# A new order, engine choice and bank choice for periods two to eight of a fused attention and channel-mix kernel

## The chip, the cores and the metric

The kernel runs on one core of a Trainium2 chip. The metric is the device time of one execution in microseconds (us). The kernel before took 204.27 us, the median of three runs (202.83 to 205.34). Engines are named as in the profile: PE (TensorE matmuls), PEld (TensorE weight loads), DVE (VectorE), ACT (ScalarE), POOL (GpSimd) and SP (SyncE, which here only issues DMAs).

## What is computed

Eight batches, eight heads, 576 tokens, head size 64; then a channel mix with 512 channels and 1024 hidden ones. Without casts and reshapes:

```python
kv  = einsum('bhsd,bhse->bhde', k, v)
out = einsum('bhsd,bhde->bhse', q, kv)
x   = out / sqrt(mean(out * out, -1) + 1e-6) * g_norm      # heads side by side: (8, 576, 512)
xk  = mu_k * x + (1 - mu_k) * x_prev                       # x_prev: one token earlier, zeros first
xr  = mu_r * x + (1 - mu_r) * x_prev
kk  = maximum(xk @ w_k, 0)
result = sigmoid(xr @ w_r) * ((kk * kk) @ w_v)
```

## The kernel before, in words

The work is cut into small steps, and the table ORDER at the top of the file writes out their order by hand, in eight strings that I call periods. Each word of it is one step: a name, its numbers (batch first), after `=` the PSUM banks that it takes, and a stroke `'` if VectorE does its elementwise part instead of ScalarE. The loop at line 760 runs through the words and emits the instructions; each engine executes its own in that order, waiting only for the data and the buffers it needs. So a word's place fixes its place in every queue at once. The first period (batches 0 and 1 in a special form) is not touched by the change.

The steps of one batch a, with their lines:

- `ld` issues the loads of k, v and q on POOL. `kv` (L292) makes k times v in 72 small matmuls; `kvo` copies the result out of PSUM, `kvs` makes a second copy with halves swapped. For batch 2 `qt` (L335, 36 transposes each, two of them) turns q on TensorE; from batch 3 on `qd` (L307) does it by DMA on SP.
- `u` (L357 for batch 2, L321 after) multiplies q with kv. For batch 2 it is 40 small matmuls (16, 8 and 16), later 72. `sq`, `red`, `nw` and `mul` are the norm: squares on ACT (L362), two sums on DVE (L366), eight tiny Newton steps on DVE (L375 to L388), five products on DVE (L398).
- `x` and `x0` (L413, 36 transposes) turn the result; `xo` and `x0o` copy it out (L403 on ACT, L405 on DVE). `wrap`, `dif` (DVE), `sc` (L579 ACT, L581 DVE) and `add` (L596, DVE) make xk (`add.a.0.h`) and xr (`add.a.1.h`).
- `K.b.f.h` (L609) is a quarter-bank group of four matmuls of 288 columns for hidden chunk f and half h; `Kp` is the same for batches 0 and 1 with other cuts. Both put a copy with relu into `rt` (L601 ACT, L603 DVE). `ks` and `ksp` square it into `sqk` (L615 ACT, L617 DVE).
- `R` (L631) is four matmuls of 512 columns and a sigmoid on ACT (L634). `V.b.t.p` (L641) is half p of the last product, four matmuls of 512 columns. `fin` (L654, DVE) multiplies both and issues two output DMAs on SP (L657). `L` is the last tile in two halves.

A matmul is two instructions for TensorE, a weight load and the multiplication. From ORDER and the loops one can count them: 516 up to the end of the first period (12 of them a warm-up), 2483 in all, so 4966 instructions besides the few that only wait. The eight PSUM banks are handed out by ORDER too: a step that takes a bank waits until its last reader is done.

Of the kernel before, what the change touches and what calls it, by code (L numbers as in the profile page):

```python
# [45 lines left out]
    R.1.5=5 Kp.1.1.3=1 ksp.1.1.2.4 red.2.5.9 red.2.0.5 nw.2.0.1 R.1.4=4 nw.2.1.2 nw.2.2.3 nw.2.3.4 R.1.8=5  # L46
    nw.2.4.5 R.1.6=1 V.1.5.0=4 ksp.1.1.4.6 nw.2.5.6 nw.2.6.7 qd.3.0 nw.2.7.8 Kp.1.1.6=5 ld.2.5 mul.2.0.1 R.1.7=1
    V.1.4.0=3 mul.2.1.0 mul.2.2.0 kv.3=56 mul.2.1.1 kvo.3.1 mul.2.0.0 ksp.1.1.6.8' x0.2=71 x.2.0.4=20 x0o.2.0
    V.1.6.0=6 kvo.3.0' xo.2.0.4.0 xo.2.0.4.1' x0o.2.1' V.1.7.0=5 wrap.2 dif.2 V.1.6.1 sc.2.0.3 sc.2.0.1'
    sc.2.0.0' add.2.0.0 sc.2.0.2 add.2.0.1 kvs.3.0 ld.0.5 V.1.4.1 ld.1.5 V.1.7.1 qd.4.1 sc.2.1.2' qd.4.0  # L50
# [4 lines left out]
    K.2.0.1=3 add.2.1.1 fin.1.5 K.2.7.0=0 add.2.1.0 K.2.6.0'=1 ld.2.6 u.3.2=2 sq.3.2.0 u.3.0=65 u.3.1=73  # L55
    sq.3.0.1 K.2.4.0'=0 sq.3.0.0 sq.3.1.1 red.3.5.9 sq.3.1.0 R.2.2=4 K.2.2.1=1 R.2.1=0 ks.2.0 K.2.7.1=4 R.2.0=1
    red.3.0.5 nw.3.0.1 K.2.1.0=0 nw.3.1.2 nw.3.2.3 nw.3.3.4 K.2.1.1=4 nw.3.4.5 ks.2.3 nw.3.5.6 nw.3.6.7
    K.2.4.1=1 nw.3.7.8 mul.3.1.0 ks.2.2 K.2.6.1=0 V.1.8.0=4 mul.3.2.0 ks.2.1 ks.2.4 V.1.8.1 mul.3.1.1 ks.2.6
# [7 lines left out]
    K.3.6.0=7 nw.4.2.3 K.3.7.1=6 K.3.2.0=1 sc.3.1.1' nw.4.3.4 K.3.1.0=7 ks.3.4 ks.3.7 nw.4.4.5 nw.4.5.6 nw.4.6.7  # L66
    nw.4.7.8 K.3.0.1=6 K.3.2.1=1 mul.4.2.0 mul.4.0.0 sc.3.1.0' V.2.3.0=7 K.3.3.0=0 K.3.6.1=6 mul.4.0.1 sc.3.1.3'
    K.3.5.0=2 mul.4.1.1 mul.4.1.0 K.3.3.1=1 sc.3.1.2' kv.5=04 add.3.1.0 ks.3.3 ks.3.2 x0.4=63 add.3.1.1 kvo.5.0
    kvo.5.1 x.4.0.4=21 ks.3.1 xo.4.0.4.1' kvs.5.0 K.3.5.1=5 x0o.4.1 xo.4.0.4.0 kvs.5.1' V.2.3.1 R.3.7=0 ks.3.6'
    x0o.4.0' fin.2.3 ld.2.7 u.5.2=4 u.5.1=15 ks.3.5 ks.3.0' ld.0.7 wrap.4 dif.4 u.5.0=63 sq.5.0.0 R.3.4=7  # L70
    sc.4.0.3' sq.5.0.1 sq.5.2.0 sc.4.1.3' sq.5.1.1 V.3.4.0=2 R.3.5=0 sq.5.1.0 red.5.5.9 sc.4.0.2 V.3.4.1
    sc.4.1.1 V.3.7.0=7 R.3.8=0 fin.3.4 sc.4.0.1' R.3.6=2 red.5.0.5 V.3.7.1 add.4.0.1 nw.5.0.1 nw.5.1.2 nw.5.2.3
    sc.4.0.0 sc.4.1.2 nw.5.3.4 ld.1.7 add.4.0.0 nw.5.4.5 fin.3.7 sc.4.1.0 nw.5.5.6 nw.5.6.7 V.3.5.0=0 V.3.6.0=2
    nw.5.7.8 add.4.1.1 mul.5.2.0 V.3.6.1 qd.6.0
# [3 lines left out]
    K.4.1.1=3 K.4.1.0'=7 fin.3.6 add.4.1.0 x0.5=14 x0o.5.1' x0o.5.0 x.5.0.4=65 ks.4.2 kv.6=37 K.4.5.1'=1  # L78
    xo.5.0.4.1 V.3.8.0=2 kvo.6.1 K.4.0.0'=4 wrap.5 xo.5.0.4.0 K.4.6.0=5 kvo.6.0 K.4.4.1=7 dif.5 K.4.4.0'=1
    K.4.5.0=6 kvs.6.1 K.4.7.0'=4 K.4.6.1'=5 fin.3.5 kvs.6.0 sc.5.0.2 sc.5.0.1 ks.4.1' sc.5.0.3' R.4.1=3  # L80
    K.4.0.1=7 ks.4.4' K.4.7.1=6 sc.5.1.3' ks.4.6 ks.4.0' ks.4.3' sc.5.1.0' sc.5.0.0 u.6.0=14 ks.4.5' add.5.0.0
    u.6.2=5 u.6.1=03 sq.6.0.1 sq.6.2.0 V.3.8.1 R.4.0=7 sq.6.1.0 ks.4.7' sq.6.1.1 sq.6.0.0 sc.5.1.1 add.5.0.1
# [3 lines left out]
    K.5.7.0'=7 K.5.7.1=2 K.5.1.0=6 K.5.6.0=7 K.5.6.1=2 red.6.5.9 red.6.0.5 nw.6.0.1 nw.6.1.2 nw.6.2.3 K.5.5.0=6
    R.4.3=7 K.5.3.1=2 nw.6.3.4 nw.6.4.5 nw.6.5.6 K.5.4.1=6 nw.6.6.7 nw.6.7.8 V.4.1.0=7 K.5.2.0=2 mul.6.0.0
    R.4.2=6 K.5.3.0=1 mul.6.1.0 mul.6.2.0 mul.6.0.1 V.4.1.1 x0.6=20 ks.5.6 sc.5.1.2 kv.7=56 mul.6.1.1 x.6.0.4=41
    qd.7.0 ks.5.7' add.5.1.0 xo.6.0.4.0 K.5.0.0=3 kvo.7.0 x0o.6.0' xo.6.0.4.1' x0o.6.1 wrap.6 V.4.2.0=2 kvo.7.1
    add.5.1.1 dif.6 sc.6.1.2' kvs.7.1 K.5.5.1=1 sc.6.0.1' K.5.1.1=4 kvs.7.0' sc.6.0.2 K.5.0.1=3 ks.5.0 R.5.4=5  # L90
    fin.4.1 sc.6.1.1' V.4.2.1 sc.6.0.3' sc.6.1.3' u.7.2=0 sc.6.0.0' sq.7.2.0 u.7.0=61 fin.4.2 sq.7.0.1 u.7.1=43
    V.4.3.0=7 V.4.3.1 sq.7.1.0 add.6.0.0 sq.7.1.1 fin.4.3 sq.7.0.0 K.5.2.1=5 R.5.5=2 R.5.8=7 add.6.0.1 ks.5.3
    red.7.0.5
# [4 lines left out]
    nw.7.5.6 V.5.8.1 nw.7.6.7 K.6.2.0=2 nw.7.7.8 K.6.0.1=7 mul.7.0.1 K.6.7.1=1 mul.7.0.0 fin.5.8 mul.7.1.1
    mul.7.2.0 mul.7.1.0 V.5.4.0=6 K.6.5.0'=2 add.6.1.1 V.5.4.1 x0.7=57 x.7.0.4=30 x0o.7.1 xo.7.0.4.1 ks.6.4
    xo.7.0.4.0' wrap.7 x0o.7.0 dif.7 ks.6.0' sc.7.0.2' R.6.2=1 sc.7.0.3' sc.7.0.0' V.5.7.0=4 sc.7.0.1 K.6.7.0=2  # L100
    add.7.0.0 K.6.2.1'=7 K.6.1.1'=3 K.6.6.1=0 V.5.5.0=5 V.5.6.0=1 K.6.1.0=2 fin.5.4 ks.6.2 add.7.0.1 sc.7.1.3
    R.5.6=0 V.5.7.1 V.5.5.1 sc.7.1.1' ks.6.1' V.5.6.1
# [2 lines left out]
    K.7.5.0'=7 sc.7.1.0' sc.7.1.2' ks.6.6 ks.6.3' K.7.1.1=3 K.7.0.0'=2 K.7.5.1=6 K.7.4.0'=0 K.7.6.1'=7 ks.6.5'
    ks.7.5' K.7.2.0'=3 K.7.0.1=2 ks.7.0 K.7.7.0'=6 K.7.7.1=0 K.7.4.1=7 ks.6.7 fin.5.7 K.7.1.0'=2 K.7.2.1'=3
    ks.7.1 add.7.1.0 V.6.1.0=6 V.6.0.0=0 V.6.3.0=4 R.6.0=7 add.7.1.1 V.6.3.1 ks.7.4' R.7.6=2 V.6.0.1 K.7.3.1=3
    V.6.2.0=7 K.7.3.0=2 V.6.1.1 ks.7.2 R.6.3=3 K.7.6.0=2 ks.7.3' fin.5.5 ks.7.7' fin.6.0 V.6.2.1 V.7.7.0=5
    R.7.4=3 fin.6.2 ks.7.6 fin.6.3 V.7.5.0=0 R.6.1=2 R.7.5=7 fin.6.1 R.7.7=4 V.7.6.0=3 V.7.7.1 fin.5.6 fin.7.7
# [685 lines left out]
```

## Time and profile before

| what | value |
|---|---|
| median of three runs | 204.27 us (202.83, 204.27, 205.34) |
| the profiled execution | 203.0 us, of which 201.2 us is the span from first to last instruction |
| PE busy | 187.9 us, 93% of the span |
| DVE, ACT busy | 157.3 us and 137.1 us |
| DMA moved | 30.14 MB |

A page row gives tenths of busy time in 40 slices of about 5 us. A row of the timeline is: start, length, engine, line, operation, tiles, shapes, number of instructions merged, and in brackets the idle time before it with what ended it ("issue" means that nothing the profile shows was missing). A row of the windows view gives a stretch, its length, then for each engine in the order PE, PEld, DVE, ACT, POOL the busy time with the count of instructions, then TensorE's granted clock, the DMA engines' share and GB/s. A row of the groups gives count, busy time, mean ns of one, and idle time before. A row of a DMA queue gives packets, megabytes and share.

### The profile page before, as it was taken

To read this page: it belongs to the slowest core of one execution; us is meant where nothing else is said; L and a number is where in the kernel's file an instruction comes from. 1 tells how busy PE (TensorE), PEld (TensorE's weight loads), DVE (VectorE), ACT (ScalarE), POOL (GpSimd) and SP (SyncE) were. 2 spreads that over 40 slices of the span, in tenths; PEclk is the share of its full clock that TensorE was granted. 3 is DMA by queue.
4 is the path that set the end of the run, shared out by engine and by line. 5 is a ranking of instruction groups with operands and counts; after the bars stand their busy time and mean duration, and the time that the engine had idled before them with its cause. 6 is when DMAs were issued, how large, how long until landed. Compare 5 with 4: busy or idle time off the path is not lost.

```text
span 201.2 us, 5937 instructions
## 1 busy us (share of the span) xinstructions
PE 187.9 (93%) x2457; PEld 113.5 (56%) x2483; DVE 157.3 (78%) x344; ACT 137.1 (68%) x287; POOL 27.1 (13%) x44
## 2 busy tenths in 40 slices
PE   7689999995999999899999999999999999999991
...
DVE  1499997986799999989989879998998777606350
...
DMA  6999999999999999999999962340422020205685
GB/s 215 213 204 207 202 207 209 206 229 208 261 186 167 189 191 260 221 184 176 229 217 199 144 144 52 81 87 3 101 60 52 3 51 1 55 2 120 154 176 124
DMA packets 33262, 30.14 MB, mean 150 GB/s; under 512 B 13644, under 2 KB 28244, under 8 KB 33236
## 3 DMA queue, kind: packets, MB, share of 16 engines
...
q14 instruction: 7, 0.06, 0.1%
...
## 4 chain that ended last, share of the span: by engine, by line
PE 78%; DMA 12%; issue 3%; POOL 3%; ACT 2%; DVE 0%; POOLq 0%
PE ps_v L641 28%; PE ps_km L609 27%; PE ps_r L631 15%; DMA wv_sb<-in_moe_w_v_dram 6%; DMA wk_sb<-in_moe_w_k_dram 5%; PE ps_u L321 2%; PE ps_x L413 2%; PE ps_kv L292 2%; ACT sqk L615 1%; POOL rt L185 1%; PE ps_v L649 1%; POOL q L185 1%; POOL wk_sb L211 1%; PE ps_u L357 1%; PE ps_qt L335 0%
## 5 line engine op out<-in xcount | busy, mean ns | idle before, releaser
L641 PE MATMUL ps_v<-wv_sb,sqk 128*128 128x512 bf16 x261 | 65.1, 379 | 1.5 <-issue 0.3
L609 PE MATMUL ps_km<-xk,wk_sb 128*128 128x288 bf16 (+3 forms) x480 | 65.3, 285 | 0.1
L609 PEld LDWEIGHTS <-wk_sb 128*128 128x128 bf16 x480 | 45.9, 98 | 17.8
L601 ACT ACTIVATE rt<-ps_km 128x288 bf16<-128x288 f32 (+3 forms) x94 | 39.3, 427 | 18.7 <-PE ps_km L609 15.3
L641 PEld LDWEIGHTS <-sqk 128*128 128x128 bf16 x280 | 26.7, 98 | 28.6 <-DVE sqk L617 0.4
L631 PE MATMUL ps_r<-wr_sb,xr 128*128 128x512 bf16 x139 | 35.2, 379 | 0.3
L634 ACT ACTIVATE sig<-ps_r 128x512 bf16<-128x512 f32 x36 | 21.5, 602 | 16.9 <-PE ps_r L631 16.7
L654 DVE TENSOR_TENSOR out_sb<-ps_v,sig 128x512 f32<-128x512 f32 (+1 forms) x37 | 24.3, 671 | 8.4 <-ACT sig L634 2.8
L631 PEld LDWEIGHTS <-xr 128*128 128x128 bf16 x144 | 13.8, 98 | 14.0
L615 ACT ACTIVATE sqk<-rt 128x576 bf16<-128x576 bf16 (+2 forms) x30 | 20.9, 710 | 0.2
L579 ACT ACTIVATE m<-dx,cols 128x576 bf16<-128x576 bf16 (+1 forms) x24 | 17.8, 767 | 3.9 <-DVE dx L573 3.8
L617 DVE TENSOR_TENSOR sqk<-rt 128x576 bf16<-128x576 bf16 (+4 forms) x27 | 13.6, 508 | 6.5 <-ACT rt L601 6.4
L603 DVE TENSOR_SCALAR rt<-ps_km 128x288 bf16<-128x288 f32 (+3 forms) x26 | 12.0, 469 | 7.9 <-PE ps_km L609 7.7
L398 DVE TENSOR_TENSOR y<-ps_u,rs 128x512 bf16<-128x512 f32 (+1 forms) x30 | 17.1, 630 | 0.2
L362 ACT ACTIVATE sq<-ps_u 128x512 bf16<-128x512 f32 (+1 forms) x30 | 14.6, 571 | 3.1 <-PE ps_u L357 2.8
L366 DVE TENSOR_REDUCE ss<-sq 128x16 f32<-128x1024 bf16 (+1 forms) x12 | 15.8, 1344 | 0.4 <-ACT sq L362 0.4
L403 ACT ACTIVATE xT<-ps_x,cols 128x1024 bf16<-128x1024 bf16 (+3 forms) x19 | 12.3, 661 | 5.4 <-PE ps_x L413 5.3
L581 DVE TENSOR_SCALAR m<-dx,cols 128x576 bf16<-128x576 bf16 (+3 forms) x42 | 13.5, 354 | 0.2
L573 DVE TENSOR_TENSOR dx<-xT 128x2304 bf16<-128x2304 bf16 (+5 forms) x13 | 11.6, 896 | 1.3 <-ACT xT L403 0.8
L596 DVE TENSOR_TENSOR xr<-m,xT 128x1152 bf16<-128x1152 bf16 x16 | 11.9, 751 | 0.1
L596 DVE TENSOR_TENSOR xk<-m,xT 128x1152 bf16<-128x1152 bf16 (+2 forms) x16 | 11.1, 701 | 0.6 <-ACT m L579 0.2
L266 PE MATMUL ps_warm<-zeros 128*128 128x512 bf16 x22 | 7.3, 458 | 1.5 <-DVE eps L229 1.2
...
## 6 DMA issues: line engine op xcount, KB each, us to landing
...
```

What stands on the lines that cost most here:

```text
L362: ACT.activation(out=sq[:, rg(t0, n, i) if n else slice(0, 1)], in_=held["u", a, part, i][1], func=AF.Square)
L366: DVE.tensor_reduce(out=ss[:, g0:g1], in_=sq[:, g0:g1], op=ALU.add, axis=AX.X)
L398: DVE.tensor_mul(out=y[:, g], in0=give(("u", a, part, i)), in1=rs[:, g].unsqueeze(3).to_broadcast([128, max(n, 1), NHP, HD]))
L579: eng.activation(out=out_, in_=in_, func=AF.Copy, scale=mu)
L596: DVE.tensor_add(out=dst, in0=m[:, hs, c0:c1], in1=x[:, hs, c0:c1])
L601: eng.activation(out=dst, in_=ps, func=AF.Relu)
L609: nc.tensor.matmul(ps[:, n, :], wk_sb[:, cc, 128 * fc:128 * fc + 128], at[b]["xk"][:, cc, c0:c1], start=(cc == 0), stop=(cc == NHP - 1))
L615: eng.activation(out=sqk[:, fcs, o:o + n], in_=src, func=AF.Square)
L631: nc.tensor.matmul(ps, xr[:, cc, 128 * t:128 * t + 128], wr_sb[:, cc, :], start=(cc == 0), stop=(cc == NHP - 1))
L634: ACT.activation(out=sig[b, t], in_=give("r"), func=AF.Sigmoid)
L641: nc.tensor.matmul(ps, sqk[:, fc, 128 * t:128 * t + 128], wv_sb[:, fc, :], start=(fc == 0), stop=(fc == NFC - 1))
L654: DVE.tensor_mul(out=o, in0=give(key), in1=sig[b, t][:, c])
```

## The change

All words of the first period stay. In periods two to eight the same words appear in another order, with other banks, and some with the other engine. No word is added or removed over the whole, and no function is changed. Four more `kvo` and one more `kvs` go from ACT to DVE, three more `ks` too; one `ksp` and one `K` go from DVE to ACT. Across the period borders some steps move later: most of the norm of batch 5, `R.3.6`, six `V` words and two `fin` words from period four to five, among others. The strings of periods two to five, whose words the prediction uses:

```diff
-    sc.1.0.3.0.384 Kp.1.0.2=5 sc.1.0.0.0.384 R.0.3=0 Kp.1.0.1=7 sc.1.1.1' Kp.1.0.0=3 sc.1.0.2.0.384'
-    add.1.0.1.0.384 Kp.1.0.3=2 add.1.0.0.0.384 Vq.0.3.3 Kp.1.1.7=5 sc.1.1.2' Kp.1.1.1=0 ld.2.3 sc.1.1.3' ld.0.3
-    ld.1.3 Kp.1.1.0=7 kv.2=32 qt.2.0=50 add.1.1.1 sc.1.1.0' kvo.2.0 kvo.2.1 add.1.1.0 ksp.1.0.0.8' qt.2.1=73
-    qto.2.0.0 qto.2.1.0 Kp.1.1.4=2 ld.2.4 ld.0.4 Kp.1.1.5=5 qto.2.0.1' ld.1.4 qto.2.1.1' fin.0.2 fin.0.1 fin.0.3
-    u.2.0=03 ksp.1.1.0.2' u.2.2=7 sq.2.2.0 qd.3.1 sq.2.0.1 u.2.1=62 Kp.1.1.2'=4 sq.2.0.0 sq.2.1.1 sq.2.1.0
...
+    sc.1.0.3.0.384' sc.1.1.1 sc.1.0.0.0.384' Vq.0.3.3 Kp.1.0.3=5 Kp.1.0.2=0 sc.1.0.2.0.384' Kp.1.0.0=7 sc.1.1.0
+    add.1.0.1.0.384 R.0.3=3 sc.1.1.2' sc.1.1.3' kv.2=25 add.1.0.0.0.384 kvo.2.1 Kp.1.1.1=0 kvo.2.0' Kp.1.0.1=7
+    add.1.1.0 ld.2.3 ld.0.3 Kp.1.1.0=3 add.1.1.1 qt.2.0=52 qto.2.0.0 qt.2.1=07 ld.1.3 ld.2.4 qto.2.1.0 ld.0.4
+    ld.1.4 fin.0.1 qto.2.0.1' Kp.1.1.2=4 qto.2.1.1' Kp.1.1.7=3 u.2.2=2 u.2.1=57 qd.3.0 ksp.1.1.0.2' ksp.1.0.0.8'
+    fin.0.2 sq.2.1.1 u.2.0=04 fin.0.3 sq.2.2.0 sq.2.1.0 Kp.1.1.6'=3 red.2.0.5 sq.2.0.0 sq.2.0.1 Kp.1.1.5=6
+    Kp.1.1.4=1 qd.3.1 red.2.5.9 Kp.1.1.3=3 R.1.6=6 R.1.7=1 nw.2.0.1 nw.2.1.2 nw.2.2.3 nw.2.3.4 nw.2.4.5
...
-    K.2.5.1=7 kvs.3.1' sc.2.1.3 K.2.3.0=0 K.2.5.0'=1 ks.2.5' sc.2.1.1' fin.1.7 K.2.0.0=2 K.2.3.1=6 K.2.2.0=7
...
-    u.4.0=24 qd.5.0 u.4.2=0 sq.4.0.0 sq.4.2.0 qd.5.1 sc.3.0.1' sc.3.0.2 sc.3.0.0' u.4.1=53 V.2.1.1 sq.4.0.1
-    sq.4.1.1 sq.4.1.0 V.2.2.0=7 add.3.0.0 fin.2.0 add.3.0.1 V.2.2.1
+    K.2.1.0=0 K.2.1.1=7 sc.2.1.3' kvs.3.0 K.2.3.1=1 K.2.3.0=6 fin.1.5 K.2.0.0=3 qd.4.1 add.2.1.0 K.2.0.1=0
...
+    sc.3.0.0' V.2.0.0=3 sc.3.1.1' V.2.0.1 kvs.4.1' sc.3.0.3 sc.3.0.1 ld.1.6 kvs.4.0 sc.3.1.0 sc.3.0.2' add.3.0.1
+    u.4.2=2 u.4.0=47 fin.2.1 sc.3.1.3' qd.5.1 add.3.0.0 u.4.1=16 fin.2.2 sq.4.2.0 fin.2.0
...
-    K.3.7.0=6 fin.2.1 fin.2.2 K.3.4.0=1 red.4.0.5 red.4.5.9 K.3.0.0=7 nw.4.0.1 nw.4.1.2 K.3.4.1=6 K.3.1.1=1
...
+    K.3.6.0'=0 sq.4.0.0 sq.4.0.1 qd.5.0 sq.4.1.0 K.3.3.0=5 sq.4.1.1 K.3.7.1=3 K.3.2.0=0 red.4.5.9 R.2.3=5
+    K.3.4.0=3 K.3.1.0=0 red.4.0.5 K.3.3.1=5 K.3.2.1=3 nw.4.0.1 nw.4.1.2 K.3.4.1=0 sc.3.1.2' nw.4.2.3 nw.4.3.4
+    nw.4.4.5 ks.3.3 nw.4.5.6 K.3.5.1=5 K.3.7.0=3 nw.4.6.7 nw.4.7.8 mul.4.1.0 V.2.3.0=0 K.3.6.1=1 K.3.0.0=5
+    mul.4.0.0 ld.2.7 mul.4.2.0 x0.4=34 ks.3.4 ks.3.7 mul.4.0.1 kv.5=27 mul.4.1.1 ks.3.2' x.4.0.4=16 kvo.5.0'
+    x0o.4.0' ld.0.7 add.3.1.0 add.3.1.1 xo.4.0.4.1 kvo.5.1' xo.4.0.4.0 K.3.0.1=5 wrap.4 x0o.4.1 K.3.1.1'=2
+    kvs.5.0 ks.3.1 ks.3.6' V.2.3.1 K.3.5.0=3 fin.2.3 dif.4 ks.3.0 R.3.8=6 R.3.5=7 sc.4.0.2' sc.4.0.0' R.3.4=2
+    R.3.7=1 sc.4.0.3' sc.4.0.1' ks.3.5 kvs.5.1' add.4.0.1 V.3.4.0=5 u.5.0=40 add.4.0.0 sq.5.0.1 sc.4.1.0'
+    sq.5.0.0 u.5.1=36 sq.5.1.1 u.5.2=7
...
-    K.4.3.1=7 V.3.5.1 qd.7.1 mul.5.0.0 K.4.2.1=7 mul.5.0.1 mul.5.1.0 mul.5.1.1 K.4.2.0=4 qd.6.1 K.4.3.0=6
...
+    K.4.3.1=2 sq.5.1.0 sc.4.1.3' V.3.4.1 K.4.1.0=1 K.4.7.0=2 fin.3.4 red.5.5.9 sq.5.2.0 red.5.0.5 nw.5.0.1
...
+    K.4.5.0=5 nw.5.6.7 ks.4.6' K.4.1.1=1 nw.5.7.8 K.4.3.0=2 V.3.6.0=5 qd.7.0 K.4.0.0=1 mul.5.1.0 mul.5.0.0
+    mul.5.1.1 ks.4.5' ks.4.1 mul.5.0.1 K.4.0.1'=3 K.4.2.1=2 sc.4.1.1' sc.4.1.2' V.3.6.1 ld.1.7 add.4.1.0
+    K.4.2.0=4 qd.6.1 mul.5.2.0 x.5.0.4=61 kv.6=02 xo.5.0.4.1 qd.6.0 kvo.6.0 x0.5=34 x0o.5.0 xo.5.0.4.0'
+    V.3.5.0=7 fin.3.6 V.3.8.0=6 x0o.5.1 wrap.5 kvo.6.1 ks.4.0 V.3.7.0=1 ks.4.2 add.4.1.1 dif.5 ks.4.3' sc.5.1.0
...
```

More of the change, by code (lines that the diff above doesn't have):

```diff
@@ L46 @@
[L46 to L50, printed above, removed]
@@ L51 @@
-    sc.2.1.0 fin.1.6 V.1.5.1 fin.1.4
-    """,
-    """
-    K.2.5.1=7 kvs.3.1' sc.2.1.3 K.2.3.0=0 K.2.5.0'=1 ks.2.5' sc.2.1.1' fin.1.7 K.2.0.0=2 K.2.3.1=6 K.2.2.0=7
[L55 to L58, printed above, removed]
@@ L59 @@
-    kv.4=71 kvo.4.1 mul.3.0.1 mul.3.0.0 ld.0.6 x0.3=23 kvo.4.0' ks.2.7' x.3.0.4=05 ld.1.6 x0o.3.0' fin.1.8
-    V.2.0.0=6 xo.3.0.4.0 kvs.4.0' xo.3.0.4.1' R.2.3=7 x0o.3.1' wrap.3 dif.3 kvs.4.1 V.2.0.1 sc.3.0.3 V.2.1.0=1
-    u.4.0=24 qd.5.0 u.4.2=0 sq.4.0.0 sq.4.2.0 qd.5.1 sc.3.0.1' sc.3.0.2 sc.3.0.0' u.4.1=53 V.2.1.1 sq.4.0.1
-    sq.4.1.1 sq.4.1.0 V.2.2.0=7 add.3.0.0 fin.2.0 add.3.0.1 V.2.2.1
-    """,
-    """
-    K.3.7.0=6 fin.2.1 fin.2.2 K.3.4.0=1 red.4.0.5 red.4.5.9 K.3.0.0=7 nw.4.0.1 nw.4.1.2 K.3.4.1=6 K.3.1.1=1
@@ L66 @@
[L66 to L74, printed above, removed]
-    """,
-    """
-    K.4.3.1=7 V.3.5.1 qd.7.1 mul.5.0.0 K.4.2.1=7 mul.5.0.1 mul.5.1.0 mul.5.1.1 K.4.2.0=4 qd.6.1 K.4.3.0=6
@@ L78 @@
[L78 to L82, printed above, removed]
@@ L83 @@
-    V.4.0.0=6 fin.3.8 V.4.0.1 fin.4.0
-    """,
-    """
[L86 to L93, printed above, removed]
-    """,
-    """
-    K.6.4.0'=5 red.7.5.9 nw.7.0.1 K.6.3.1=2 ks.5.2 K.6.3.0'=7 ks.5.1' nw.7.1.2 K.5.4.0=5 R.5.7=2 sc.6.1.0'
-    nw.7.2.3 ks.5.5' K.6.6.0=5 K.6.5.1=7 ks.5.4 K.6.0.0=2 nw.7.3.4 nw.7.4.5 add.6.1.0 V.5.8.0=5 K.6.4.1=7
@@ L98 @@
[L98 to L102, printed above, removed]
-    """,
@@ L104 @@
-    """
[L105 to L109, printed above, removed]
@@ L110 @@
-    V.7.4.0=2 V.7.6.1 V.7.4.1 fin.7.6 fin.7.4 V.7.5.1 R.7.8=6 fin.7.5 L.0=7 L.1=1 wm.1=4
+    sc.1.0.3.0.384' sc.1.1.1 sc.1.0.0.0.384' Vq.0.3.3 Kp.1.0.3=5 Kp.1.0.2=0 sc.1.0.2.0.384' Kp.1.0.0=7 sc.1.1.0
+    add.1.0.1.0.384 R.0.3=3 sc.1.1.2' sc.1.1.3' kv.2=25 add.1.0.0.0.384 kvo.2.1 Kp.1.1.1=0 kvo.2.0' Kp.1.0.1=7
+    add.1.1.0 ld.2.3 ld.0.3 Kp.1.1.0=3 add.1.1.1 qt.2.0=52 qto.2.0.0 qt.2.1=07 ld.1.3 ld.2.4 qto.2.1.0 ld.0.4
+    ld.1.4 fin.0.1 qto.2.0.1' Kp.1.1.2=4 qto.2.1.1' Kp.1.1.7=3 u.2.2=2 u.2.1=57 qd.3.0 ksp.1.1.0.2' ksp.1.0.0.8'
```

45 lines of the change are left out of this document (added).

## The prediction

> **What bounds the kernel now.** I read the page first: which engine is full, and where it has a hole.
>
> ```profile
> span 201.2 us, 5937 instructions
> PE 187.9 (93%) x2457; PEld 113.5 (56%) x2483; DVE 157.3 (78%) x344; ACT 137.1 (68%) x287; POOL 27.1 (13%) x44
> PE   7689999995999999899999999999999999999991
> DVE  1499997986799999989989879998998777606350
> DMA  6999999999999999999999962340422020205685
> ```
>
> PE is full from slice 4 to the end, except for the 5 in slice 10 and an 8 in slice 17. DVE is nearly as full up to slice 30. The change leaves the first period and the set of instructions alone, so it can win only what PE now loses after about 38 us. The list of PE's waits says how much that is:
>
> ```profile
> PE ps_u L357 <- issue: 2.5, 1, 2.5
> PE ps_u L321 <- PE ps_u L321: 0.8, 1, 0.8
> ```
>
> All other PE waits there are 0.2 us or less. Neither of the two has a releaser in another engine. The timeline shows where they are, inside a row of equal matmuls:
>
> ```profile
> 44.15 0.67 PEld L292 LDWEIGHTS <-sq 64*64 64x64 bf16 x72 [0.32 <-issue]
> 47.10 0.38 PE L357 MATMUL ps_u<-kv,qT 64*128 64x64 bf16 x14
> 49.97 0.78 PE L357 MATMUL ps_u<-kv,qT 64*128 64x64 bf16 x26 [2.50 <-issue]
> 84.56 0.57 PE L321 MATMUL ps_u<-kv,qT 64*64 64x64 bf16 x40 [0.76 <-PE ps_u L321]
> 100.11 0.50 PEld L321 LDWEIGHTS <-qT 64*64 64x64 bf16 x52 [0.19 <-issue]
> ```
>
> PE stops after 14 of the 16 matmuls of `u.2.0`, which all wait for the same data: no data can be missing there. The third stop, 0.19 us, is at 100.11. How many weight loads lie between the stops?
>
> ```profile
> 49.97:84.55 34.58, 33.50 (x506) 19.90 (x511) 30.86 (x66) 27.51 (x55) 4.47 (x6) 1.00 1.18 209
> 84.56:100.10 15.54, 15.21 (x253) 10.43 (x255) 14.46 (x31) 13.46 (x32) 2.22 (x3) 1.00 1.15 203
> ```
>
> 511 and 255 in the second bracket: 4 x 128 and 2 x 128, less one. A load comes with a matmul, so PE stops at multiples of 256 instructions: it waits for its own code. The DMA view, asked for stretches of 0.1 us from 47.6, 54.1, 82.0 and 117.5, holds one packet of the instruction queue each time:
>
> ```profile
> q8 instruction: 1, 0.02, 60.9%
> q8 instruction: 1, 0.02, 59.2%
> q8 instruction: 1, 0.02, 59.3%
> q8 instruction: 1, 0.02, 106.8%
> ```
>
> 60.9% of 16 engines in 0.1 us is 0.97 us for one packet. `u.2.0` begins with load 718 by ORDER, so the stop is at load 732 and pieces begin at 604, 732, 860 and so on. Load 604 is number 38 of `kv.2`, at 44.5 (first row of the timeline). So the next piece starts to travel 3.1 us after the piece before it was entered, takes 1.0, and PE goes on 1.4 later, at 49.97: 5.5 us from entry. The one at 82.0 gives 3.4 and 5.9 (entry 78.7), the one at 54.1 a lag of 4.2 (entry 50.0). At 117.5 the lag is negative, entry 118.6: there the DMA row has fallen from 9 to 6 and 2. **The rule of this trace**: while the DMA engines are full, a piece that holds less than 4 to 6.5 us of PE work ends in a stop. After about 115 us it doesn't matter.
>
> [...]
>
> **The change, part by part.** First the code pieces. Durations of PE groups, from the chain that ended last:
>
> ```profile
> 38.33 0.66 PE ps_km L609 x8
> 44.93 0.83 PE ps_qt L335 x72
> 56.48 0.65 PE ps_km L609 x4
> 57.99 0.86 PE ps_v L641 x4
> 58.86 0.71 PE ps_kv L292 x72
> 72.13 0.49 PE ps_km L609 x4
> 156.18 0.63 PE ps_x L413 x36
> ```
>
> Piece 604 to 732 before: the rest of `kv.2` 0.33, two `qt` 0.83, two `Kp` 1.30, 14 of `u` 0.38, together 2.8. It lasted 5.5, hence 2.50 lost. In the new order `kv.2` stands earlier and this piece holds: 14 loads of `kv.2` 0.14, `Kp.1.1.1`, `Kp.1.0.1`, `Kp.1.1.0`, `Kp.1.1.2` and `Kp.1.1.7` at 0.65, 0.83 of `qt`, 18 of `u` 0.49 (0.027 each): 4.7. Against 5.5 to 5.9 that leaves a stop of 0.8 to 1.2; I take 0.9. Bounds: 0 if the code comes as soon as at 117.5, 1.9 with the lag of 4.2 (4.2 + 1.0 + 1.4 - 4.7).
>
> The other short pieces by the same sums: 1116 to 1243 goes from 5.0 to 7.3 and 1370 to 1498 from 3.9 to 7.8, so their 0.76 and 0.19 go. 1626 to 1754 goes from 4.5 to 4.3 (three `K` 1.47, `V` 0.86, `x` with `x0` 0.63, `kv` 0.71, three quarters of a `V` 0.65), but it comes at about 111, when the loads are nearly through: 0, at most 4.2 + 1.0 + 1.4 - 4.3 = 2.3. So code costs 3.45 before and 0.9 after (0 to 4.2): **2.55 won**.
>
> Second, what the earlier PE runs into. `kv.2` moves up from 44.2 to about 41.6 (38.3, where the first period's `R` end, and one `Vq` 0.43, three `Kp` 1.98, one `R` 0.86). Its v was issued here and needs this long to land, so it is there at 39.8; no cost, 1.8 us in hand. The adds for `Kp.1.1.1` end near 41.6 by DVE's rows and PE asks at 42.3: covered.
>
> ```profile
> 25.19 0.74 POOL L196 DMA_DIRECT2D qT<-in_v_dram  x1 [1.90 <-DMA wv_sb<-in_moe_w_v_dram]
> DMA to landing us min/median/max: 14.6/14.6/14.6
> ```
>
> The transposes `qd` keep SP busy for microseconds, and outputs queue behind them. In the new order `qd.3.0` stands behind one output pair and not three, so batch 3's come earlier; `qd.4` and `qd.5` move behind `fin.1.5` and `fin.2.1`, but `u.4` and `u.5` then follow 15 us or more later, as before. POOL's loads keep their order. I cost both at 0; the cover is that distance.
>
> Small bank waits are new: `R.1.6` takes bank 6 two groups after `Kp.1.1.5`, whose copy stands on ACT behind five squares; `K.3.7.1` takes bank 3 right behind `fin.2.0`. My sums of the rows put ACT or DVE 0.1 to 0.2 behind PE there: 0.2 together (0 to 0.5).
>
> Third, DVE. From the last `add.a.0` of one batch to the next one's, DVE works through one turn, and the first `K` of the next batch waits for it. Rows for that:
>
> ```profile
> L654 DVE TENSOR_TENSOR out_sb<-ps_v,sig 128x512 f32<-128x512 f32 x35 | 23.5, 685 | 6.9 <-ACT sig L634 2.8 <-PE ps_v L641 2.3 <-issue 1.6
> L398 DVE TENSOR_TENSOR y<-ps_u,rs 128x512 bf16<-128x512 f32 x24 | 15.5, 683 | 0.1
> L581 DVE TENSOR_SCALAR m<-dx,cols 128x576 bf16<-128x576 bf16 x33 | 11.1, 364 | 0.1
> L596 DVE TENSOR_TENSOR xr<-m,xT 128x1152 bf16<-128x1152 bf16 x14 | 10.3, 751 | 0.1
> L603 DVE TENSOR_SCALAR rt<-ps_km 128x288 bf16<-128x288 f32 x23 | 10.2, 455 | 4.9 <-PE ps_km L609 4.7
> L617 DVE TENSOR_TENSOR sqk<-rt 128x576 bf16<-128x576 bf16 x21 | 9.3, 452 | 6.5 <-ACT rt L601 6.4
> L366 DVE TENSOR_REDUCE ss<-sq 128x20 f32<-128x1280 bf16 x6 | 8.9, 1477 | 0.0
> L573 DVE TENSOR_TENSOR dx<-xT 128x2304 bf16<-128x2304 bf16 x6 | 8.2, 1358 | 1.2 <-ACT xT L403 0.8
> L366 DVE TENSOR_REDUCE ss<-sq 128x16 f32<-128x1024 bf16 x6 | 7.3, 1211 | 0.4 <-ACT sq L362 0.4
> L403 ACT ACTIVATE xT<-ps_x,cols 128x1024 bf16<-128x1024 bf16 x7 | 7.8, 1116 | 0.8 <-PE ps_x L413 0.7
> L388 DVE SCALAR_TENSOR_TENSOR rs<-ns,rs 128x36 f32<-128x36 f32 x12 | 2.3, 195 | 0.4
> 46.21 1.88 DVE L654 TENSOR_TENSOR out_sb<-ps_v,sig 128x512 f32<-128x512 f32 x3
> 64.00:101.00 37.00, 35.69 (x623) 23.60 (x628) 34.48 (x75) 31.63 (x69) 6.70 (x9) 1.00 1.16 203
> ```
>
> The turn from batch 3 to 4 in the new order: three `fin` 2.06, two `K` 0.91, two `red` 2.69, eight `nw` 1.5, five `sc` 1.82, five `mul` about 3.15, two `ks` 0.90, four `add` 3.0, `dif` 1.36, and 1.35 of copies: 18.7 in 37 instructions. Neighbours overlap (three `fin` take 1.88 and not 2.06, 0.09 each; 0 where one needs the other); with 0.05 each it is 16.9. PE has 16.9 in the same turn (16 `K`, 5 `R`, 3 `V`, `u`, `x`, `kv`). Room: 0. The tightest turn before, batch 4 to 5, has 17.4 less 1.7 against 16.1 of PE, room 0.4, and shows no wait of PE. The other new turns have 1.5, 1.2, 1.2 and 1.0, the old ones 1.5, 1.4, 1.1 and 2.8. DVE also has waits of its own in a turn, above all `wrap` for ACT's two `xo` of 1.12: in the stretch from 64 to 101 it was idle 2.5 us in nearly two turns. By that, 1.2 a turn, the new order would lose 1.2 + 0.2 + 0.2 = 1.6; if they fit into the room as in the tight old turn, 0. I take the middle, **0.8 lost** (0 to 5, below), most of it at `K.4.3.1`.
>
> At the end nothing changes: 30 us of `V`, `R` and `K` are left for PE with half as much for DVE, and the last tile and its output are the same steps.
>
> **The sum.** -3.45 + 0.9 + 0.2 + 0.8 = -1.55. The profiled execution took 203.0 us, so 201.5; that execution was 1.3 under the median of 204.27, and on the scale of medians it is 202.7.
>
> **The rivals.**
> - Everything is won: the code arrives in time and DVE keeps up, 204.27 - 3.45 = 200.8. For it: the stop at 100.11 cost only 0.19 with 3.9 us of work in its piece, so the lag there was about 1.7 (3.9 + 0.2 - 1.0 - 1.4). Against: in the place that counts, 44 to 50 us, it was 3.1, and DVE has no room in one turn.
> - The code comes no better: the piece at 604 meets the lag of 4.2 (now `qd.3.0` travels just there) and the one at 1626 still finds loads and transposes under way. Then 1.9 + 2.3 = 4.2 is lost for 3.45, and 1.0 besides: 206.0. For it: `qd.7.0`, `qd.6.1` and `qd.6.0` start around 105 to 112. Against: only two pieces are short.
> - The stops aren't for code at all and stay where the work is: 204.27 + 1.0 = 205.3. Against it stand the counts 511 and 255. [...]
> - **The other side**: DVE becomes the bound. With `wrap` and its like costing 2.0 a turn, the rooms of 1.5, 0, 1.2, 1.2 and 1.0 leave 0.5 + 2.0 + 0.8 + 0.8 + 1.0 = 5.1, and 204.27 - 3.45 + 0.9 + 0.2 + 5.1 = 207.0. It decides from 1.5 us of such waits a turn, where the loss of about 2.4 eats the gain. For it: 1.2 to 1.3 is measured, and DVE takes eight steps over from ACT and gives two back. Against: part of that idle time was there because PE was late.
>
> **How the numbers follow.** Forecast 0.54, all won 0.14, code no better 0.10, not code 0.04, DVE bound 0.18. The predicted time is the likeliest case's, 202.7; its own range is 201.3 to 204.3. From the 200.8 of all won to the lower half of the DVE case the range is 200.7 to 205.9, leaving about 2 in 10 out. A measurement of this kernel tells about 2% from no change, 4.1 us: faster means under 200.2, which needs all won and a fast set of runs, 0.06; slower means over 208.4, the far end of the DVE case, 0.08; within, 0.86.
>
> **What would show it.** Right: the 2.50 in PE's waits becomes about 1 and stands in `u.2.1`, the stop in `u.4` is gone, `K.4.3.1` waits for DVE's add for less than 1. Wrong: a PE wait of 2 us or more at a multiple of 128 loads near 48 or 114, waits of `K` for `add` in three turns, or PE halts inside `u` that don't sit at such multiples.

## The result, and the profile after

The changed kernel took 202.44 us (median of 20 runs, 201.01 to 206.65), the kernel before beside it 204.25 us (20 runs, 202.63 to 207.08): a ratio of 0.9911, with a 95% interval of 0.9884 to 0.9938. That is 1.8 us or 0.9% less: a small gain, less than the 2% that the prediction named as the least change it could tell. The prediction was 202.7, so the number is right. Not every step of it is.

The ratios here and below leave out executions more than 1.5% above the fastest of their kernel, so they need not equal the quotient of the medians, and the profiled execution of the changed kernel is one of those left out (205.45 us, span 203.6). From its page, rows that were shown of before, and the granted clock of TensorE (PEclk):

```profile
PE   7889999997999999999969999999999999999991
DVE  1499987987998799999908998899998991547340
PEclk9999999999999999999979999999999999999999
```

The 5 that PE had in slice 10 is a 7, and the 8 in slice 17 is gone. New in slice 21 are a 6 for PE, a 0 for DVE and a 7 in the granted clock. The timeline of PE in the same execution has the places (start, duration, then what PE idled just before):

```profile
35.70 2.75 PE L630 MATMUL ps_r<-wr_sb,xr 128*128 128x512 bf16 x12
...
46.59 0.56 PE L356 MATMUL ps_u<-kv,qT 64*64 64x64 bf16 x18
48.26 0.49 PE L356 MATMUL ps_u<-kv,qT 64*128 64x64 bf16 x22 [1.11 <-issue]
...
103.62 0.85 PE L320 MATMUL ps_u<-kv,qT 64*64 64x64 bf16 x72 [2.29 <-DMA qT<-in_q]
...
119.79 2.53 PE L640 MATMUL ps_v<-wv_sb,sqk 128*128 128x512 bf16 x11 [0.32 <-issue]
...
196.96 1.91 PE L648 MATMUL ps_v<-wv_sb,sqk 128*128 128x256 bf16 x16
```

The stop of 1.11 is the forecast one: after 18 matmuls of `u`, in `u.2.1`, at the boundary at load 732. The stops in `u.4` and at 100 us are gone. The 0.32 at 119.79 is the boundary behind the piece 1626 to 1754. The 2.29 was not in the forecast: `u.5.0` waits for its DMA transposes. (`u.5.0` starts a few loads ahead of the boundary at 1498, so code would be a rival. But in e6 below the boundary is 88 loads away and `u.5` still waits 1.06, and in e4 the boundary is where it was and the wait is gone.) The clock around it stands in the table of windows (length, busy time of PE, PEld, DVE, ACT and POOL, granted clock, DMA share, GB/s):

```profile
64.00:101.00 37.00, 37.00 (x566) 23.69 (x563) 34.63 (x74) 32.44 (x71) 4.46 (x6) 1.00 1.20 185
...
100.00:105.00 5.00, 2.71 (x82) 1.55 (x80) 2.26 (x6) 2.74 (x6) 0.90 (x2) 0.94 0.87 204
105.00:110.00 5.00, 5.00 (x28) 3.02 (x27) 2.48 (x3) 3.29 (x9) 1.33 (x2) 0.71 0.99 150
```

Up to 101 us PE is full, 37.00 of 37.00 where it was 35.69 before. Then it stands for 2.29 us, and for the next 5 us it gets 0.71 of the clock, by which I estimate 5 x 0.29 = 1.45 more.

To take the accounts free of the first period, which the change leaves alone, I measure each profile from the row of the first period's last twelve `R` matmuls to the row of the last sixteen matmuls. After, these are the first and the last row of the timeline above; before:

```profile
35.58 2.75 PE L631 MATMUL ps_r<-wr_sb,xr 128*128 128x512 bf16 x12
...
194.67 1.91 PE L649 MATMUL ps_v<-wv_sb,sqk 128*128 128x256 bf16 x16
```

159.09 before, 161.26 after: 2.17 longer in this execution. By its rows: -3.45 (the old stops) + 1.11 + 0.32 + 2.29 + 1.45 + 5 x 0.06 (the clock of 0.94) = 2.02. So the rows account for it to 0.15, and without the wait in `u.5.0` and its clock it would be 1.9 shorter than before (2.17 - 2.29 - 1.45 - 0.30). Whether that wait belongs to the change is a question for experiments.

### The profile page after: what moved, and what is told of

It is laid out like the page before. It is cut to its first block, busy times and chain, and to the rows that moved or that the text cites. A ratio compares the mean times of both kernels' runs of the same rounds, so it can differ in the third digit from the quotient of the medians.

```text
span 203.6 us, 5959 instructions
## 1 busy us (share of the span) xinstructions
PE 192.3 (94%) x2483; PEld 114.0 (56%) x2483; DVE 157.7 (77%) x350; ACT 134.8 (66%) x281; POOL 27.2 (13%) x44
## 4 chain that ended last, share of the span: by engine, by line
PE 69%; DMA 11%; DVE 10%; issue 3%; ACT 2%; POOL 1%; SPq 0%; DVEq 0%; POOLq 0%
PE ps_v L640 25%; PE ps_km L608 23%; PE ps_r L630 12%; DMA qT<-in_q 6%; DMA rt<-in_v_dram 4%; PE ps_km L680 2%; DVE ss L365 2%; PE ps_x L412 2%; DVE out_sb L653 2%; PE ps_u L320 1%; PE ps_kv L291 1%; DMA out_dram<-out_sb 1%; ACT sq L361 1%; DVE y L397 1%; PE ps_qt L334 1%
## 5 line engine op out<-in xcount | busy, mean ns | idle before, releaser
L640 PE MATMUL ps_v<-wv_sb,sqk 128*128 128x512 bf16 x280 | 68.3, 383 | 0.6 <-issue 0.3
L608 PE MATMUL ps_km<-xk,wk_sb 128*128 128x288 bf16 (+3 forms) x480 | 66.9, 288 | 0.0
L633 ACT ACTIVATE sig<-ps_r 128x512 bf16<-128x512 f32 x36 | 21.0, 598 | 20.8 <-PE ps_r L630 20.7
L602 DVE TENSOR_SCALAR rt<-ps_km 128x288 bf16<-128x288 f32 (+3 forms) x25 | 11.5, 468 | 12.3 <-PE ps_km L608 12.1
L578 ACT ACTIVATE m<-dx,cols 128x576 bf16<-128x576 bf16 x24 | 17.9, 768 | 3.4 <-DVE dx L572 3.3
L614 ACT ACTIVATE sqk<-rt 128x576 bf16<-128x576 bf16 (+2 forms) x28 | 19.6, 718 | 0.1
L365 DVE TENSOR_REDUCE ss<-sq 128x20 f32<-128x1280 bf16 (+1 forms) x12 | 16.0, 1348 | 0.4 <-ACT sq L361 0.2
L616 DVE TENSOR_TENSOR sqk<-rt 128x576 bf16<-128x576 bf16 (+4 forms) x29 | 14.3, 501 | 0.5 <-ACT rt L600 0.5
L265 PE MATMUL ps_warm<-zeros 128*128 128x512 bf16 x24 | 8.4, 484 | 1.2 <-DVE eps L228 1.2
```

Source lines behind the costliest of these rows:

```text
L365: DVE.tensor_reduce(out=ss[:, g0:g1], in_=sq[:, g0:g1], op=ALU.add, axis=AX.X)
L578: eng.activation(out=out_, in_=in_, func=AF.Copy, scale=mu)
L608: nc.tensor.matmul(ps[:, n, :], wk_sb[:, cc, 128 * fc:128 * fc + 128], at[b]["xk"][:, cc, c0:c1], start=(cc == 0), stop=(cc == NHP - 1))
L614: eng.activation(out=sqk[:, fcs, o:o + n], in_=src, func=AF.Square)
L633: ACT.activation(out=sig[b, t], in_=give("r"), func=AF.Sigmoid)
L640: nc.tensor.matmul(ps, sqk[:, fc, 128 * t:128 * t + 128], wv_sb[:, fc, :], start=(fc == 0), stop=(fc == NFC - 1))
```

## The experiments

Theory A: the gain is that of the code pieces alone. Which stops there are follows from where the boundaries of 256 instructions fall, not from order, banks or engines, and a later place of batch 5's transposes costs some of it. Rivals: the stops follow the work or its waits; PE takes stops back later because DVE sets its pace; the transposes' wait is chance.

**The changed kernel again (e1), no edit.**

> The changed kernel once more, beside the kernel before on one chip. Theory A (the gain is the code's arrival; the batch-5 wait for the DMA transposes of 2.3 us is in every run): ratio 0.99, and this profile again shows a stop of about 1.1 us at load 732 in u.2.1 and a wait of u.5 for the transposes of about 2 us. Theory B (the wait for the transposes belongs to the one profiled execution only): same ratio, and this profile shows the stop of 1.1 but no wait of u.5.

Measured: 203.09 us, ratio 0.9951 (0.9909 to 0.9994), somewhat above the 0.9911 of the first measurement, with intervals that overlap. PE's waits, then its timeline with the issue of `qd.5.0` from SP's:

```profile
PE ps_kv L449 <- DMA rt<-in_v_dram: 1.8, 1, 1.8
...
PE ps_u L356 <- issue: 1.1, 1, 1.1
PE ps_u L320 <- DMA qT<-q: 0.6, 1, 0.6
```

```profile
38.43 2.76 PE L630 MATMUL ps_r<-wr_sb,xr 128*128 128x512 bf16 x12
...
93.69 4.63 SPq L306 DMA_TRANSPOSE qT<-in_q  x1
...
104.13 0.85 PE L320 MATMUL ps_u<-kv,qT 64*64 64x64 bf16 x72
...
196.08 1.91 PE L648 MATMUL ps_v<-wv_sb,sqk 128*128 128x256 bf16 x16
```

The 1.1 in `u.2.1` is there again, the wait in `u.5` is not. But the first period took 2.7 us longer here (38.43 against 35.70; PE waited 1.8 us for v), so PE asked later. From `R` to the end it is 157.65, 1.44 less than before. By waits: 1.1 for code and 0.6 in `u.6` for `qT`, 1.7 in place of 3.45: -1.75. At the boundary behind 1626 to 1754 PE doesn't stop here; 0.3 of the account stays open.

**Only the cutting, in the kernel before (e2 and e3).** Small matmuls that nothing reads take the place of some of the twelve of the kernel's `warm(12)`, so all later instructions move on by 64 or 24 pairs of load and matmul:

```diff
-    warm(12)
+    warm(9)
+    ps = take("warm", [128, C], FP32, "ps_warm")
+    for n in range(67):
+        nc.tensor.matmul(ps[half(n % 2), :64], zeros[half(n % 2), :64], zeros[half(n % 2), :64], start=True, stop=True)
+    give("warm")
```

(e3: `warm(11)` and 25.)

> The order of before, untouched; only the warm-up at the start, while PE waits for data anyway, is 9 wide and 67 tiny matmuls instead of 12 wide ones, so every later instruction stands 128 places further (64 pairs) and the pieces of code are cut elsewhere. Theory A (stops are the code's arrival, fixed to the cutting): the stops in u.2.0, u.4 and u.5 of 2.50, 0.76 and 0.19 us go; the one short piece is then loads 540 to 668 (4.4 us of PE work, among the qt), a stop of about 1.1 us; 2.2 us won, ratio 0.989. Rival (the stops belong to the place in the order, or the gain of the change comes from its order as such): the stops stay in u.2.0 and u.4, ratio 1.00.

> The same with 24 pairs instead of 64. Theory A: the piece from load 580 to 708 then holds 1.4 us of work (rest of kv.2, qt.2.0 and most of qt.2.1), so PE stops for about 4 us inside qt.2.1, and for about 0.7 near u.4 and up to 1.5 near 114 us; 1 to 2.5 us slower than before, ratio 1.005 to 1.012. Rival: stops stay in u.2.0 and u.4, ratio 1.00.

Measured: e2 201.12 us, ratio 0.9862 (0.9819 to 0.9905); e3 204.69 us, ratio 1.004 (1.001 to 1.007). PE's timeline of e2, then two rows of e3's:

```profile
36.40 2.75 PE L631 MATMUL ps_r<-wr_sb,xr 128*128 128x512 bf16 x12
...
192.88 1.91 PE L649 MATMUL ps_v<-wv_sb,sqk 128*128 128x256 bf16 x16
```

```profile
48.46 0.22 PE L335 MATMUL ps_qt<-ident,q 64*64 64x64 bf16 x2 [2.44 <-issue]
...
100.22 1.04 PE L631 MATMUL ps_r<-wr_sb,xr 128*128 128x512 bf16 x4 [1.68 <-DVE sqk L617]
```

In e2, with not one word of ORDER changed, the three stops are gone and `R` to end is 156.48, 2.61 less than before: at least as much as the whole change wins. The stop of 1.1 that I had expected at the new boundary among the `qt`, behind a piece of 4.4 us, did not come either. In e3 `u.2.0` and `u.4` run through, and instead PE stops in `qt.2.1` (2.44; I had expected about 4) and at `R.3.7` (1.68). The second is put down to DVE, but it sits at a moved boundary (old load 1474; the trace has 1499 loads before it, 24 of them new); I read it as a code stop under another releaser's name. 2.44 + 1.68 = 4.1 against 3.45 is 0.7 us or 0.3% more; measured 0.4%, a little under the 0.5 to 1.2% expected.

**Control: a whole piece more (e7).** `warm(6)` and 134 small matmuls, 128 pairs more, so that each step lies in its piece as before.

> Control for e2: the kernel before with 128 pairs more (one whole piece), so that every later step lies in its piece as before, while the start has more of the small matmuls than e2. Theory A (the cutting decides): 204.3 us, ratio 1.000, stops of about 2.5 us in u.2.0 and 0.8 us in u.4 are back. Theory C (the small matmuls at the start help in some other way, a warmer clock or a later start): as e2 or better, ratio 0.986 or less.

Measured: 205.31 us, ratio 1.0048 (1.0026 to 1.007). PE's waits and timeline:

```profile
PE ps_u L357 <- issue: 2.7, 1, 2.7
PE ps_qt L459 <- issue: 1.3, 1, 1.3
```

```profile
38.09 2.75 PE L631 MATMUL ps_r<-wr_sb,xr 128*128 128x512 bf16 x12
...
196.95 1.91 PE L649 MATMUL ps_v<-wv_sb,sqk 128*128 128x256 bf16 x16
```

The stop in `u.2.0` is back, a stop of 0.5 in `u.4` (0.76 before) too, and `R` to end is 158.86 (before 159.09). So the small matmuls as such don't help later; the boundaries do. The 1.3 is new: it stands at the early boundary near load 220, which now falls a few us behind the small matmuls (they end at 7.3, PE stops at 10.0), so that by my reading the next piece comes late in the first period. Around it the clock is 0.83 from 10 to 20 us (1.00 before), and `R` starts 2.51 later than in the profile of before; measured is a loss of 0.5%.

**The changed kernel, cut badly (e8).** `warm(10)` and 42 small ones: 40 pairs more.

> The changed kernel cut badly: 40 pairs more put boundaries at the old loads 564, 692, 1332 and 1460, so the piece 564 to 692 holds 3.2 us of PE work and the piece 1332 to 1460 holds 4.2 us. Theory A: a stop of 1.7 to 2.9 us in qt.2.1, one of about 1.4 us in K.3.0.1, none in u.2.1: 203.1 + 2.7 = 205.8 us, ratio about 1.007, that is the gain of the change is lost though its order, banks and engines are all there. Theory C: as e1 or better, ratio 0.995 or less.

Measured: 206.4 us (203.76 to 210.07), ratio 1.0053 (1.0018 to 1.0088). Timeline of PE, and one row of SP, in a profiled execution of 210.07 us:

```profile
47.20 0.31 PE L334 MATMUL ps_qt<-ident,q 64*64 64x64 bf16 x14 [1.56 <-issue]
...
53.10 9.53 SPq L306 DMA_TRANSPOSE qT<-in_q  x1
...
73.53 1.15 PE L320 MATMUL ps_u<-kv,qT 64*64 64x64 bf16 x64 [4.67 <-DMA qT<-in_q]
...
103.21 1.14 PE L608 MATMUL ps_km<-xk,wk_sb 128*128 128x288 bf16 x8 [1.36 <-ACT xT L402]
```

The new order, banks and engines are all there, and the gain isn't. Both stops stand where the cut puts them (1.56 in `qt.2.1`, 1.36 at `K.3.0.1`, put down to ACT but with 1499 loads before it, as in e3). The 4.67 in `u.3` was in no expectation: the second of batch 3's transposes, `qd.3.1`, which this order issues behind four outputs as well, was issued at 53.10 and landed only by 73.5. No other profile has that wait.

**Batch 5's transposes earlier (e4).**

```diff
-    mul.3.0.0 ks.2.4 mul.3.0.1 R.2.1=7 x0.3=25 kv.4=16 ks.2.6' fin.1.8 x0o.3.1 x.3.0.4=43 ks.2.3 xo.3.0.4.0
+    mul.3.0.0 ks.2.4 mul.3.0.1 R.2.1=7 x0.3=25 kv.4=16 ks.2.6' fin.1.8 qd.5.1 qd.5.0 x0o.3.1 x.3.0.4=43 ks.2.3 xo.3.0.4.0
```

(and the two words taken out further on.)

> The changed kernel with the two transposes of batch 5 moved up in the order, from behind fin.2.1 and fin.2.0 to right behind fin.1.8. Theory A (u.5's wait is in every run): they land near 95 us instead of 103.6, u.5 doesn't wait, 2 us more are won than by the change alone, ratio 0.980. Theory B (only in the one execution): ratio as the change alone, 0.991.

Measured: 200.98 us (200.47 to 201.88), ratio 0.9854 (0.9818 to 0.989), between the two theories; it is the lowest of all, with e2 (0.9862) within its interval. Timelines of PE and, where marked, SP and POOL, of e4; then the same places of the changed kernel and of the kernel before (there the last row is the first of `u.5`):

```profile
35.54 2.76 PE L630 MATMUL ps_r<-wr_sb,xr 128*128 128x512 bf16 x12
...
79.23 7.24 SPq L306 DMA_TRANSPOSE qT<-in_q  x2
...
84.26 0.87 PE L320 MATMUL ps_u<-kv,qT 64*64 64x64 bf16 x72 [0.27 <-DMA qT<-q]
...
101.47 0.85 PE L320 MATMUL ps_u<-kv,qT 64*64 64x64 bf16 x72
...
192.66 1.91 PE L648 MATMUL ps_v<-wv_sb,sqk 128*128 128x256 bf16 x16
```

```profile
87.33 3.57 SPq L656 DMA_DIRECT2D out_dram<-out_sb  x4
90.95 7.65 SPq L306 DMA_TRANSPOSE qT<-in_q  x1
...
104.10 0.74 POOL L195 DMA_DIRECT2D in_q<-in_q_dram  x1 [17.59 <-DMA qT<-in_q]
```

```profile
81.97 9.98 SPq L307 DMA_TRANSPOSE qT<-in_q  x2
...
97.24 0.74 POOL L196 DMA_DIRECT2D in_q<-in_q_dram  x1 [16.18 <-DMA qT<-in_q]
...
99.62 1.09 PE L321 MATMUL ps_u<-kv,qT 64*64 64x64 bf16 x72
```

POOL's load into the buffer that the transposes read starts when they are done, so it dates their landing: before at 97.2, 2.4 us ahead of `u.5` at 99.6. In the changed kernel `qd.5.0` is issued at 90.95, behind four outputs, and is done by 103.6, when `u.5` starts, while PE is ready at 101.3: nothing is in hand. In e1 the issue is at 93.69 and PE asks at 104.13, just late enough. In e4 `u.5` has no wait. `R` to end is 157.12: -1.97, against -3.45 + 1.12 + 0.27 = -2.06 by its one code stop (1.12 in `u.2.1`, as in e1) and the wait in `u.4`.

**The transposes later in the kernel before (e9), the mirror.** `qd.5.0` alone behind `fin.2.2`.

> The mirror of e4: the kernel before, with qd.5.0 alone moved behind fin.2.2, so that on SP it stands behind six outputs instead of none. Theory A (the place of batch 5's transposes costs time by itself): it starts about 90.5 us instead of 84.3, lands near 103 with the 12.7 us from issue to landing that both profiles showed, and u.5, which PE reaches at 100, waits 2 to 4 us: ratio 1.01 to 1.015, 206.5 to 207.5 us. Theory B (the place is covered): no PE wait for qT in u.5, ratio 1.000.

Measured: 204.39 us, ratio 1.0015 (0.9984 to 1.0045): no cost, theory A's 2 to 4 us are missing. The timelines of SP, POOL and PE, and a window behind the stop in `u.2.0`:

```profile
92.54 2.86 SPq L307 DMA_TRANSPOSE qT<-in_q  x1
...
99.56 0.74 POOL L196 DMA_DIRECT2D in_q<-in_q_dram  x1 [16.71 <-DMA qT<-in_q]
101.16 0.82 PE L321 MATMUL ps_u<-kv,qT 64*64 64x64 bf16 x72
```

```profile
50.00:55.00 5.00, 4.71 (x39) 2.41 (x41) 3.08 (x3) 3.10 (x7) 0.00 (x0) 0.66 1.16 263
```

The issue did move, from 82.0 to 92.5, but here the transposes need 7.0 from the last issue to landing, not 12.7. They land at 99.56, when PE asked in the profile of before (99.62); here PE asks 1.5 later. So the late place costs nothing here, but takes away the cover, and a wait comes where their time, 7 to 12.7 us, is long. PE's delay arises before they are issued: `R` to end is 160.49 (35.45 to 195.94), 1.40 longer than before, and the clock behind the stop in `u.2.0` (2.72 here) is 0.66 for 5 us, 5 x 0.34 = 1.7 us by my estimate.

**The changed kernel without short pieces (e5, e6, e10, e11).** 88 pairs more: by my sums no piece before 112 us then holds under 5.6 us of PE work. e5 has e4's edit as well (`warm(8)` and 92 small matmuls), e6 hasn't (`warm(9)` and 91).

> Both costs left in the changed kernel are taken away at once: batch 5's DMA transposes stand earlier (as in e4), and the numbering of TensorE's instructions is moved on by 88 pairs, so that no piece of 256 before 112 us holds under 5.6 us of PE work. Theory A (the stops are for code, and the order's gain and the transposes' cost are separate terms): the 1.1 us in u.2.1 and some 0.4 us in the piece at load 1626 go, 201.0 - 1.5 = 199.5 us, ratio to the kernel before 0.977, and no PE wait from issue above 0.3 us after 40 us. Theory B (PE takes such stops back later, since DVE and ACT set its pace): as e4, 201.0 us, ratio 0.985.

> The numbering alone, with batch 5's transposes where the change put them. Theory A: 203.1 - 1.5 = 201.6 us, ratio 0.988, no stop in u.2.1; u.5 may still wait for its DMA transposes (0 to 2.3 us), and this kernel stays about 2 us above e5. If the transposes' place costs nothing by itself and e4 was faster for another reason, e5 and e6 are equal.

Measured: e5 201.71 us, ratio 0.986 (0.9819 to 0.990); e6 204.89 us (201.74 to 208.54), ratio 0.9954 (0.9913 to 0.9996). Theory A's 0.977 and 0.988 did not come, and by totals its rival, that PE takes the stops back, would have it. PE's timeline of e5, with its window from 10 to 20 us, and rows of e6 in an execution of 205.02 us:

```profile
12.40 0.44 PE L449 MATMUL ps_kv<-rt 64*64 64x64 bf16 x15 [1.31 <-issue]
...
38.09 2.75 PE L630 MATMUL ps_r<-wr_sb,xr 128*128 128x512 bf16 x12
...
193.64 1.91 PE L648 MATMUL ps_v<-wv_sb,sqk 128*128 128x256 bf16 x16
```

```profile
10.00:20.00 10.00, 7.64 (x96) 4.28 (x84) 7.39 (x18) 6.39 (x16) 4.88 (x7) 0.83 1.22 205
```

```profile
39.95 2.75 PE L630 MATMUL ps_r<-wr_sb,xr 128*128 128x512 bf16 x12
...
105.27 0.85 PE L320 MATMUL ps_u<-kv,qT 64*64 64x64 bf16 x72 [1.06 <-DMA qT<-in_q]
...
196.59 1.91 PE L648 MATMUL ps_v<-wv_sb,sqk 128*128 128x256 bf16 x16
```

From `R` on e5 takes 155.55, 1.57 less than e4 and 3.54 less than before: the stops are gone and stay gone, as A has it (1.5 and 3.45). The time is lost before: with a new stop of 1.31 at 12.4, at the same early boundary as in e7, and a clock of 0.83 from 10 to 20 us (1.00 before), `R` starts 38.09 - 35.54 = 2.55 later than in e4. My expectation had left the first period out. e6 takes 156.64 from `R` on, 1.09 more than e5, about its wait of 1.06 in `u.5`.

e10 keeps 64 of the pairs at the start, as e2, and puts 24 behind the last `Vq.0.3.3` (bank 5); e11 also has `qd.3.1` right behind `qd.3.0`.

> e5 without its loss in the first period: 64 pairs more at the start, as in e2, and the other 24 behind the last Vq.0.3.3, where the new order has a free bank. From kv.2 on the cutting is that of e5. Theory A: e4's 201.0 less 1.5 us of stops plus 0.5 us for 24 pairs: 200.0 us, ratio 0.980, no PE wait from issue above 0.3 us after 40 us, none of 1.3 us in the first period. Theory B: as e4 and e5, 0.9855.

> e10, with qd.3.1 moved up to stand right behind qd.3.0, before four outputs, as in the kernel before. In e8's profile u.3 waited 4.7 us for these transposes; in five other profiles of the new order it did not. Theory A (their place costs only in slow stretches of the DMA): e10's median or up to 0.5 us less, 199.5 to 200.0 us, ratio 0.978 to 0.980, with less spread. Theory B (the transposes then crowd the loads and the code at 47 to 60 us): a code stop near 54 us and a ratio above e10's by 0.005.

Measured: e10 202.35 us, ratio 0.9877 (0.9832 to 0.9921); e11 201.74 us, ratio 0.9879 (0.9836 to 0.9923). Both miss. PE's timeline of e10 shows where this execution lost it:

```profile
12.71 0.64 PE L455 MATMUL ps_kv<-rt 64*64 64x64 bf16 x18 [0.78 <-DMA rt<-in_v_dram]
...
37.49 2.75 PE L636 MATMUL ps_r<-wr_sb,xr 128*128 128x512 bf16 x12
...
194.07 1.91 PE L654 MATMUL ps_v<-wv_sb,sqk 128*128 128x256 bf16 x16
```

There is no code stop in the first period now, but PE waits for v, its clock is 0.83 there again, and `R` starts 1.95 later than in e4. From `R` on it is 156.58, with some 0.5 of that in the 24 pairs. e11 tells nothing of the place of `qd.3`: equal to e10 within the interval, and no wait in `u.3` in either. Whether e10 would beat e4 with an undisturbed first period stays open.

## Why the prediction was right or wrong

- **Code, 2.55 won: right in its mechanism, a little too large.** The stop in `u.2.1` was put at 0.9 and measured 1.1 (three profiles); those in `u.4` and at 100 us went, and the piece at 1626, put at 0, gave 0.3 in one profile and nothing in e1 and e4. So 2.0 to 2.3 was won. That the order did it only through the boundaries is shown: e2 wins 2.6 us with the old order, e8 loses the gain with the new one, e7 gets the old stops back. The bound of 4 to 6.5 us is loose: a piece of 4.4 us ended without a stop in e2. e2 and e7 have the same work from `R` on, cut in other places, and are 2.4 us apart there (156.48 and 158.86). So PE waited for more than the data and the buffers that the kernel's description names: 2.50 us in `u.2.0` before, 1.11 in `u.2.1` after. That it is code is my reading: the runs show that the stops move with the numbering, and the pages' 19 instruction packets for 2483 loads before and 20 for 2611 in e7 fit it, but no row names what PE waits for.
- **DVE, 0.8 lost: wrong, 0.** The step that failed is the one that took the middle between rooms of 0 and waits of 1.2 a turn, that is, counted DVE's idle time as a loss for PE. From 64 to 101 us DVE is busy 34.63 of 37.00 us, idle nearly as long as before (2.37 against 2.52), while PE is busy all 37.00. No `K` has a wait of 0.2 us or more in the changed kernel, e4 or e5. In e5, which has neither old stops nor the wait in `u.5`, 3.54 is won against 3.45 of stops, and nothing is left for DVE.
- **Banks, 0.2: 0.** No `R` or `K` behind the first period has a wait of 0.2 us or more in these three profiles.
- **"I cost both at 0; the cover is that distance": the reason was wrong, the price is open.** The forecast named `fin.1.5` and `fin.2.1`, but `qd.5.0` also stands behind `fin.2.2` and `fin.2.0`, four outputs more on SP: it is issued at 90.95 and not near 82, and with 12.7 us to landing the distance is used up. It cost 2.3 us and a clock of 0.71 in one profile, 1.1 in e6, 0 in e1. By ratios, moving it up wins 0.0097 (e1 to e4) and 0.0094 (e6 to e5), about 2 us both times, and in neither pair do the intervals overlap. But against the first measurement of the changed kernel, 0.9911, e4 wins only 0.0057, with intervals that overlap. And in the profiles only 0.53 us (e1, e4) and 1.09 us (e6, e5) of the difference lie behind the common row; 2.89 and 1.86 us lie in the first period, which is the same in e1 and e4 and nearly so in e6 and e5; and in e1 none of the 0.53 is a wait in `u.5`. I put the price of the place at 0.5 to 2 us; how much of it is the transposes stays open. Nor did batch 3's transposes come earlier: `qd.3.1` too stands behind two more output pairs, and POOL's load that follows them starts at 67.94, against 67.83 before.
- **A term that the sum lacks: the clock behind a stop.** The prediction carried the 1.3 us between its profiled execution and the median over unchanged. e9 has the stop in `u.2.0` and behind it the clock of 0.66, about 1.7 us, which the profile of before has not. Of the 62 executions of the kernel before that the ratios of the experiments use, 44 have a mean granted clock of 0.990 or less (median 204.5 us) and 18 a higher one (203.6); of e2, without the stop, five of six have 0.997 or more. By my estimate from these a stop costs most executions more than its own length: e2 wins 1.8 us between the two profiled executions, but 3.15 by medians. That this clock is lost behind the stop in the unprofiled executions is not shown.
- **The sum** was right in part by luck: 0.8 + 0.2 for DVE and banks didn't come, which made up for 0.2 to 0.5 less from code and for the transposes, costed at 0, for which I put 0.5 to 2.
- **The rivals.** "Everything is won" is nearly what e5 shows from `R` on, but with another cut. "The code comes no better" put 1.9 and 2.3 where 1.1 and at most 0.3 were measured. "Not for code", with stops that stay where the work is, is refuted by e2, e3, e7 and e8, "DVE bound" by the rows above.
